# A long convolution with a gated block, forward and backward: transforms moved from dense products on TensorE to a radix-8 transform shared with VectorE, and one row order for all stages

## The chip, the cores and the metric

The kernel runs on one core of a Trainium2 chip. The metric is the device time of one execution in microseconds, taken as the median of several runs. When two kernels are compared, the ratio is the mean time of one kernel's fast runs over that of the other's fast runs of the same rounds on the same chip. It is therefore not quite the ratio of the medians quoted beside it.

## The reference, cut to what matters

Ten outputs: the result and nine gradients. The gradients come from automatic differentiation, so the kernel has to write out the backward pass by hand.

```python
# S = 2048 rows, D = 1024 channels, F = 3584; all bf16
def _A_ref(q, k, v, shift_k, ssm_k, ssm_D):
    k_pad = jnp.pad(k, ((0, 0), (ks - 1, 0), (0, 0)))               # ks = 4
    for t in range(ks):
        k_shift = k_shift + k_pad[:, t:t + S, :] * shift_k[:, ks - 1 - t]
    kv = k_shift * v
    y = irfft(rfft(pad(kv, 2 * S)) * rfft(pad(ssm_k, 2 * S)))[:S]     # long convolution, each channel
    return q * (y + kv * ssm_D)

def _B_ref(x, w_gate, w_up, w_down):
    h = (x @ w_gate) * (x @ w_up)
    return h @ w_down

xn = layernorm(x); s = _A_ref(xn, ...); g = silu(_B_ref(xn, ...))
out = x + s * g                                                       # and all gradients of it
```

Row t of the shifted k needs rows t-3 to t of k, and the gradient needs rows t to t+3.

## The kernel before

The transforms of the long convolution are dense products with tables of sines and cosines. They go through DRAM between forward, product and inverse. This is the inverse:

```python
for dh in range(DH):
    YSh = ys_pool.tile([P, NB2, 2, 2, 512], BF16, name="YSh")
    for gb in range(NB2):
        dma(YSh[:, gb, :, :, :], Psrc_v[gb, :, :, :, sl])
    for ub in range(NB2):
        for par in range(2):
            ps = pspool.tile([P, 512], F32, name="psI")
            for gb in range(NB2):
                for c in range(2):
                    nc.tensor.matmul(ps[:], tws2[c][:, gb * P:(gb + 1) * P], YSh[:, gb, par, c, :], ...)
```

Transposes go to one bank eight at a time, but each 128-column block is copied out by itself:

```python
for i in range(nt):
    nc.tensor.transpose(pst[:, i * P:(i + 1) * P], srcs[g0 + i], ident[:])
for i in range(nt):
    nc.any.tensor_copy(dst_fn(g0 + i), pst[:, i * P:(i + 1) * P])
```

For the shift, k is first copied to a padded array in DRAM. Each of the four taps is then its own load, shifted by a row, and each covers 128 partitions:

```python
nc.sync.dma_start(out=KPAD[0:4, :], in_=zero_bf[0:4, :])
for sb in range(NB):
    dma(KPAD[4 + sb * P:4 + (sb + 1) * P, :], kin[sb * P:(sb + 1) * P, :])
# ... later, for each block of 128 rows and each tap j:
    kt = dkp.tile([P, D], BF16, name=f"kt2_{j}")
    base_row = 4 + sb * P - j
    dma(kt[:], KPAD[base_row:base_row + P, :])
```

## Time and profile before

| | before |
|---|---|
| time | 3117 us median (3114 to 3120, 4 runs) |
| span of the profiled run | 3117.5 us |
| TensorE busy | 88% |
| VectorE / ScalarE / GpSimd busy | 52% / 34% / 20% |
| bytes moved by DMA | 627 MB in 393,008 packets |

The groups table of the page puts the costliest kinds of instruction first. The columns are line, engine, operation, output and inputs, shapes and count, then busy time and mean ns of one, then the idle time before them and what ended it:

```profile
L429 PE MATMUL psI<-YSh,TWR 128*128 128x512 bf16 x1536 | 355.9, 391 | 69.5 <-DVE TWR L217 19.1
L443 ACT COPY HH<-pst_hh 128x128 bf16<-128x128 bf16 x441 | 117.2, 266 | 50.0 <-PE pst_hh L441 38.0
```

The first line is the inverse transform shown above. It is the largest single group on TensorE, and 69.5 us of waiting come on top. The second is one of the single-block copies, 441 times 0.27 us.

### The profile page before, as it was taken

How to read it: one execution, taken by the hardware profiler on the slowest of the kernel's cores; microseconds unless marked ns; L12 is line 12 of the kernel's file. 1: busy time of each engine (PE TensorE's matmuls, PEld its weight loads, DVE VectorE, ACT ScalarE, POOL GpSimd, SP SyncE). 2: the span in 40 equal slices, each digit the busy share in tenths (PEclk: the TensorE clock that was granted, in tenths of full speed). 3: DMA queues.
4: the chain of work that ended last, by engine and by line, in shares of the span. 5: the costliest groups of instructions: out<-in, count | busy, mean ns of one | idle time of the engine just before them, and what ended most of it. 6: DMA issues, size and time to landing. Idle time of an engine off the chain costs nothing. (4 is left out here: it accounts for less than half of the span.)

```text
span 3117.5 us, 39882 instructions
## 1 busy us (share of the span) xinstructions
PE 2728.1 (88%) x13818; PEld 1281.9 (41%) x13818; DVE 1626.6 (52%) x3829; ACT 1060.1 (34%) x2938; POOL 626.8 (20%) x1049
## 2 busy tenths in 40 slices
PE   4949899999799979799899999878899599889888
PEld 2413344444344434444444444433444344444333
DVE  7977778111255751299953331184997460034461
ACT  6512433333101113545535543300555530242222
POOL 2221132222334320112110110133221111112200
PEclk8978999999899989899999999998999689889988
DMA  7795595343748882588644432266875685558602
GB/s 250 286 334 193 193 322 216 145 167 117 280 156 288 284 295 102 185 299 280 214 168 140 141 127 92 94 224 208 296 264 178 213 250 158 161 162 244 210 25 84
DMA packets 393008, 626.92 MB, mean 201 GB/s; under 512 B 147795, under 2 KB 260435, under 8 KB 388964
## 3 DMA queue, kind: packets, MB, share of 16 engines
q1 hardware_dynamic: 304406, 312.36, 30.9%
q0 software_dynamic: 88400, 312.02, 27.9%
q8 instruction: 108, 1.77, 0.2%
q14 instruction: 94, 0.77, 0.1%
HBM read 406.89 MB, written 221.55 MB: 202 GB/s over the span
## 5 line engine op out<-in xcount | busy, mean ns | idle before, releaser
L429 PE MATMUL psI<-YSh,TWR 128*128 128x512 bf16 x1536 | 355.9, 391 | 69.5 <-DVE TWR L217 19.1
L688 PE MATMUL psG<-XNT,wg_s 128*128 128x512 bf16 x896 | 342.7, 383 | 11.3 <-ACT g_b L691 6.8
L689 PE MATMUL psU<-XNT,wu_s 128*128 128x512 bf16 x896 | 342.6, 382 | 3.2 <-DMA wu_s<-in_B_w_up_dram 3.0
L1105 PE MATMUL ps_dxn<-WGT,dgt_l 128*128 128x512 bf16 x896 | 341.6, 382 | 0.0
L1105 PE MATMUL ps_dxn<-WUT,dut_l 128*128 128x512 bf16 x896 | 340.9, 381 | 0.2 <-DMA dut_l<-DUTd 0.2
L936 PEld LDWEIGHTS <-XNR 128*128 128x128 bf16 x1792 | 174.9, 98 | 212.7 <-issue 9.1
L429 PEld LDWEIGHTS <-TWR 128*128 128x128 bf16 x1536 | 152.2, 100 | 262.0 <-issue 64.5
L920 PE MATMUL ps_dh<-DBMT,WDT 128*128 128x512 bf16 x896 | 221.3, 390 | 9.8 <-ACT WDT L443 8.7
L1058 PE MATMUL ps_dwd<-DBM,HH 128*128 128x512 bf16 x896 | 206.2, 382 | 12.1 <-ACT HH L443 7.4
L936 PE MATMUL ps_dw<-DG,XNR 128*128 128x512 bf16 x896 | 199.9, 381 | 3.9 <-ACT w_b L939 3.0
L756 PE MATMUL ps_bm<-WD,ht_t 128*128 128x512 bf16 x896 | 195.7, 381 | 3.7 <-DMA ht_t<-HTd 3.7
L936 PE MATMUL ps_dw<-DU,XNR 128*128 128x512 bf16 x896 | 194.9, 379 | 1.6 <-ACT w_b L939 1.5
L695 DVE TENSOR_TENSOR h_b<-g_b,u_b 128x512 bf16<-128x512 bf16 x112 | 47.4, 423 | 225.6 <-ACT u_b L693 225.6
L939 ACT CAST w_b<-ps_dw 128x512 bf16<-128x512 f32 x112 | 65.3, 584 | 267.3 <-PE ps_dw L936 257.7
L691 ACT CAST g_b<-psG 128x512 bf16<-128x512 f32 x112 | 65.5, 585 | 256.4 <-PE psG L688 239.7
L689 PEld LDWEIGHTS <-wu_s 128*128 128x128 bf16 x896 | 88.3, 99 | 117.7 <-issue 10.8
L688 PEld LDWEIGHTS <-wg_s 128*128 128x128 bf16 x896 | 88.2, 98 | 112.3 <-issue 8.7
L443 ACT COPY HH<-pst_hh 128x128 bf16<-128x128 bf16 x441 | 117.2, 266 | 50.0 <-PE pst_hh L441 38.0
L756 PEld LDWEIGHTS <-ht_t 128*128 128x128 bf16 x896 | 87.7, 98 | 111.7 <-issue 4.6
L1105 PEld LDWEIGHTS <-dut_l 128*128 128x128 bf16 x896 | 88.0, 98 | 106.6 <-issue 1.6
L1105 PEld LDWEIGHTS <-dgt_l 128*128 128x128 bf16 x896 | 88.1, 98 | 105.2 <-issue 1.1
L1058 PEld LDWEIGHTS <-HH 128*128 128x128 bf16 x896 | 84.7, 98 | 110.8 <-ACT HH L443 15.2
(341 smaller groups left out, 4574.9 us busy)
## 6 DMA issues: line engine op xcount, KB each, us to landing
kt<-KPAD SPq DMA_DIRECT2D x64, 256.0 KB, 5.2
kt<-KPAD POOLq DMA_DIRECT2D x64, 256.0 KB, 5.0
dgt_l<-DGTd SPq DMA_DIRECT2D x16, 896.0 KB, 11.5
dut_l<-DUTd POOLq DMA_DIRECT2D x16, 896.0 KB, 8.8
dgt_l<-DGTd POOLq DMA_DIRECT2D x16, 896.0 KB, 8.4
dut_l<-DUTd SPq DMA_DIRECT2D x16, 896.0 KB, 8.1
KVFd<-kvf_t POOLq DMA_DIRECT2D x6, 1536.0 KB, 6.0
pp_kvf<-KVFd SPq DMA_DIRECT2D x12, 768.0 KB, 9.7
```

The source lines that it names most:

```text
L429: nc.tensor.matmul(ps[:], tws2[c][:, gb * P:(gb + 1) * P], YSh[:, gb, par, c, :], start=(i_mm == 0), stop=(i_mm == nmm - 1))
L443: nc.any.tensor_copy(dst_fn(g0 + i), pst[:, i * P:(i + 1) * P])
L688: nc.tensor.matmul(psG[:], wg_s[:, dc, fi * P:(fi + 1) * P], rhs, start=(dc == 0), stop=(dc == DC - 1))
L689: nc.tensor.matmul(psU[:], wu_s[:, dc, fi * P:(fi + 1) * P], rhs, start=(dc == 0), stop=(dc == DC - 1))
L691: nc.scalar.copy(out=g_b[:], in_=psG[:])
L695: nc.vector.tensor_tensor(h_b[:], g_b[:], u_b[:], ALU.mult)
L756: nc.tensor.matmul(ps[:, dh * 512:(dh + 1) * 512], lhsT, WD[:, fc, dh * 512:(dh + 1) * 512], start=(fc == 0), stop=(fc == FC - 1))
L920: nc.tensor.matmul(ps[:], WDT[:, ddc, fi * P:(fi + 1) * P], DBMT[:, ddc, cs], start=(ddc == 0), stop=(ddc == DC - 1))
L936: nc.tensor.matmul(ps[:], XNR[:, sb, dc * P:(dc + 1) * P], src[:, sb, :], start=(sb == 0), stop=(sb == NB - 1))
L939: nc.scalar.copy(out=w_b[:], in_=ps[:])
L1058: nc.tensor.matmul(pss[k][:, dh * 512:(dh + 1) * 512], HH[:, sb, fi * P:(fi + 1) * P], DBM[:, sb, dh * 512:(dh + 1) * 512], start=(sb == 0 ...
L1105: nc.tensor.matmul(ps[:], lt[:, fc, :], wt[:, fc, :], start=(i_acc == 0), stop=(i_acc == n_acc - 1))
```

## The change

The intent: take TensorE's largest non-essential work away. Rows are ordered as (half c, partition u, r of 8), so that a transform of length 4096 splits into a dense product over u (128x128 matmuls, on TensorE) and a radix-8 butterfly over r (on VectorE). All stages use that order, so nothing is reordered between them. Eight transposes fill a bank and leave it in one copy. Transforms are interleaved with dense products by a pump that hands out work in proportion. The diff has some 2,000 lines. Its core:

```diff
-    def fwd_transform2(Zs, tw_source, pspool, on_acc, on_nyq):
-        ...  nc.tensor.matmul(psA[:], twc_t[:, ub * P:(ub + 1) * P], rhs, ...)     # 512 columns
+    def fwd_unit(x, X, wp, psp, nr=2):                    # 128 channels, all 2048 rows
+        W = wp.tile([P, 20, 256], F32, name="W")
+        for h in range(4 // nr):
+            ...  nc.tensor.matmul(ps[:, 2 * i + k, g * P:(g + 1) * P], TF[:, r0 + i, c, k, ...],
+                                  x[:, 8 * c + r0 + i, :], ...)                     # 128 columns
+            nc.scalar.copy(out=s, in_=psS[:])
+            tt(W[:, n * h:n * h + n, :], s, psP[:], ADD)
+            tt(W[:, 8 + n * h:8 + n * h + n, :], s, psP[:], SUB)
+        dft_even(W, 0, W[:, 16:20, :], X, False)          # VectorE
+        dft_odd(W, 8, W[:, 16:18, :], X, False)           # VectorE
...
-            for i in range(nt):
-                nc.any.tensor_copy(dst_fn(g0 + i), pst[:, i * P:(i + 1) * P])
+            for dc in range(DC):
+                nc.tensor.transpose(ps[:, dc, :], x4[:, i, dc * P:(dc + 1) * P], ident[:])
+            nc.any.tensor_copy(XNT[q][:, :, i * P:(i + 1) * P], ps[:])
...
-        for sb in range(NB):
-            dma(KPAD[4 + sb * P:4 + (sb + 1) * P, :], kin[sb * P:(sb + 1) * P, :])
+                k = kst.tile([P, 11, 256], BF16, name="k")     # 8 rows and a halo of 3
+                if c == 0:
+                    V.memset(k[0:1, 0:3, :], 0.0)
+                    ld(k[0:1, 3:11, :], kin[0:8, d0:d0 + 256].rearrange("(o r) d -> o r d", o=1))
+                    ld(k[1:P, :, :], bass.AP(kin.tensor, kin.offset + 5 * D + d0,
+                                             [[8 * D, P - 1], [D, 11], [1, 256]]))
+                else:
+                    ld(k[:], bass.AP(kin.tensor, kin.offset + 1021 * D + d0, [[8 * D, P], [D, 11], [1, 256]]))
...
+    def dk_unit(ds, ew, psy):                              # in the w_down gradient, eight times
+        ld(kh[1:P, 0, :, :], bass.AP(kin.tensor, kin.offset + 5 * D + d0, [[8 * D, P - 1], [D, 11], [1, P]]))
+        ld(dk[0:P - 1, :, 8:11, :], src[1:P, :, 0:3, :])
...
+            nc.scalar.activation(hv[:, 2 * rp:2 * rp + 2, :], ps[:], ACT.Copy, scale=WSC)   # step of 16 bytes
```

## The prediction

> **What bounds the kernel now.** I read the page first (engine shares, the forty slices), then the table of busy time by stage with stage borders taken from the first and last start of each matmul line, then the timeline of TensorE and of VectorE for the price of one instruction. The page says:
>
> ```profile
> PE 2728.1 (88%) x13818; PEld 1281.9 (41%) x13818; DVE 1626.6 (52%) x3829; ACT 1060.1 (34%) x2938; POOL 626.8 (20%) x1049
> PE 24%; issue 8%; ACT 4%; DMA 4%; DVE 3%; POOL 1%; SPq 0%; POOLq 0%; ACTq 0%; DVEq 0%
> ```
>
> TensorE is the bound, but busy time counts overlapping pipeline ends, so I price it from the timeline instead:
>
> ```profile
> 1607.53 27.79 PE L936 MATMUL ps_dw<-DU,XNR 128*128 128x512 bf16 x128
> 1635.15 1.06 PE L441 MATMUL pst_fg<-ident,wrow 128*128 128x128 bf16 x16
> ```
>
> One 512-column matmul lasts 0.379 us alone, so 128 of them start every (27.79-0.38)/127 = 0.2158 us. A 128-column one lasts 0.219, so sixteen start every (1.06-0.22)/15 = 0.056 us. By the kernel's own order it issues about 11,270 of the first (3,168 of them in the transforms) and 2,528 of the second: 2,432+142 = 2,574 us of pure streaming in a span of 3,118. The other 544 us are waits and a slow clock, and the stage table shows where (columns: stretch, its length, busy time of PE, PEld, DVE, ACT, POOL, then granted clock, DMA share, GB/s):
>
> ```profile
> 188.00:245.00 57.00, 9.00 (x20) 2.13 (x21) 32.82 (x55) 1.15 (x2) 15.13 (x29) 0.52 0.97 358
> 390.00:800.00 410.00, 395.14 (x1824) 178.45 (x1823) 158.52 (x386) 128.54 (x248) 110.56 (x191) 0.98 0.53 189
> 940.00:1137.00 197.00, 195.57 (x896) 87.67 (x896) 136.86 (x195) 32.31 (x31) 70.75 (x132) 0.99 0.81 283
> 1297.00:2018.00 721.00, 678.05 (x3867) 331.08 (x3865) 381.94 (x1233) 334.46 (x1096) 99.00 (x166) 0.98 0.52 175
> 2437.00:2480.00 43.00, 17.89 (x117) 11.81 (x116) 22.56 (x69) 22.54 (x80) 8.65 (x10) 0.61 0.93 313
> ```
>
> The second, third and fourth rows are dense stages: 1,792 matmuls (387 us) in 410, 896 (193 us) in 197, and 643 us of work in 721. The first and last are seams, where TensorE starves while a DRAM round trip or weight transposes catch up. Six such seams sum to about 190 us. The first also shows DMA saturating at 358 GB/s, a number needed below.
>
> **What the Trainium skill says.** "TensorE: Matmul & The Clock Gate", section "Back-to-back issue gap", gives N/2.4 + 2.5 ns for a warm stream: 216 and 56 ns for 512 and 128 columns, and it adds that real load-and-multiply pairs of 128 columns take about 81 ns. The trace agrees with the first (215.8, 56) and not with the 81. For 256 columns, which the trace lacks, the formula gives an estimate of 109 ns. "VectorE: DVE Perf Modes", section "The perf-mode tier table (the rule you actually need)", lets a two-tensor operation on bf16 run at 2x and on f32 at 1x. The trace agrees (start to start 0.60 and 1.14 us for 1,024 elements):
>
> ```profile
> 2200.54 0.69 DVE L996 TENSOR_TENSOR dkprod<-dksh,Wbc 128x1024 bf16<-128x1024 bf16 x1
> 2201.14 1.22 DVE L1008 TENSOR_TENSOR acc<-acc,prodf 128x1024 f32<-128x1024 f32 x1
> 2202.28 0.69 DVE L997 TENSOR_TENSOR dkacc<-dkacc,dkprod 128x1024 bf16<-128x1024 bf16 x1
> ...
> 23.03 1.28 DVE L217 SCALAR_TENSOR_TENSOR twc_g<-S0n,SPHp,tw_tmp 128x1024 bf16<-128x1024 f32 x1
> 24.23 1.28 DVE L220 SCALAR_TENSOR_TENSOR tws_g<-C,SPHn,tw_tmp 128x1024 bf16<-128x1024 f32 x1
> ```
>
> "DMA: Bandwidth & Descriptors", section "Where 436 GB/s comes from", puts the HBM limit of one core near 358 GB/s; the saturated stretch above shows the same figure.
>
> **The change, TensorE.** The transforms go from 3,168 matmuls of 512 columns (684 us) to 1,536 forward and 1,024 inverse ones of 128 columns and 256 of 256 columns: 143+28 = 171 us. Added are 128 small matmuls for the gradient of D (7) and 128 full ones for that of the shift kernel (28). The transposes of the saved h disappear (448), but h is now transposed when it is made (448), so their number hardly moves. The dense products stay at 8,064 matmul equivalents. New total: 7,296x0.2158 + 2,048x0.109 + 5,152x0.056 = 1,575+224+288 = 2,087 us. So 487 us of streaming leave, and the seams of DRAM round trips between transforms go with them. Single-block evictions of transposes (0.27 us each on ScalarE, some 1,700) become evictions of eight (about 1.06 us per eight), so ScalarE stays under TensorE everywhere.
>
> **VectorE.** It inherits the transform. With the spacings above (0.60 us for 512 f32, 1.14 for 1,024, 2.2 for 2,048; estimates scaled: 0.40 for 256-element scalar-tensor-tensor, 1.13 for 2,048 bf16), a forward unit costs 4x1.14 + 2x1.14 + 4x0.60 + 6x0.60 + 8x0.40 + 0.3 for direct dependences = 16.3 us. An inverse costs 16.2 and a product 6.9 to 7.5.
>
> **Stages, as the build's own order shows them.** (The order is interleaved by a scheduler, so I count per stage.)
>
> First stage: layer norm, gate and up products, both forward transforms and the first inverse. TensorE: 387 + 86 (conv) + 43 (transposes) = 516 us. VectorE: eight slices of 2x16.3+6.9+16.2+2.3 = 58 us, 464 in all; shift products 64x1.13 = 73; 56 h products 34; layer norm 36; tables 18; rest 6: 631. So this stage turns from TensorE-bound to VectorE-bound. The waits: 12 us until the first operands are there; per forward unit about 2.5 us, as its work tile and its two PSUM banks are single and ScalarE's 1.0 us copy stands between matmul and add, 16 times = 40; ScalarE's queue in front of it, some 17. Sum 700 us. In the order, the last h product stands before more than a whole slice of conv work, so about 80 us at the end are VectorE alone. TensorE can put only one block of the next stage there.
>
> Middle stage: w_down product, gates, elementwise, half of the dy transforms. TensorE 193+7+14 = 215 less 16 done before; VectorE 16x6.9 + 4x16.5 = 176; but the bytes are 29.4 (h) + 7.3 (w_down) + 16.8 + 4.2 + 16.8 + 6 = 81 MB, at 358 GB/s 226 us. I take 235.
>
> Gradient stage: dh 196, dw 387, transposes 70, conv 55 = 708 us of TensorE; VectorE has 628 us over this and the next part, so it is beside. The dense stage before ran 12% over its content, mostly transposes in single blocks. I allow 9%, for the single A and B buffers whose loads come late in each of the 14 slabs: 770, plus 15 for the seam in front. Then dw_down: 193+14+28 = 235, I take 240.
>
> Last stage: 387+25, 20 for the first 7.5 MB of loads (5.5 MB of transposed gradients are queued before the first weights; at 358 GB/s 21 us), 13 for the tail of the last block: 445.
>
> Sum 700+235+785+240+445 = 2,405. For clock ramps and unplaced waits (seams cost 190 us before, I have named 35 here) I add 35: **2,440 us**, 22% less.
>
> **Rivals.** (1) The first stage locks step: VectorE waits for TensorE in queue order and TensorE for VectorE, and starved TensorE drops to half clock, as at 188 to 245 us (0.52). For it: single-buffered PSUM and work tiles. Against: the order has already moved other work into many of the gaps. It would cost 16x6 = about 100 us more: 2,540. (2) The scheduler's order hides all waits: first stage 660, gradient stage 735: 2,340 or a little below. (3) The middle stage and gradient stage are DMA-bound by small pieces: 256- and 512-byte runs in the new layouts. For it: 81 MB in 230 us is already the ceiling, and the kernel before moved its 627 MB with a third of its packets under 512 B. Against: the new h blocks are 14 KB per partition. 10% less rate costs 25 us there: 2,465. (4) VectorE's transform costs more than it saves, and nothing is gained: this would need VectorE's instructions to be twice as long as measured. I give this almost nothing.
>
> **Range and chances.** Rivals 1 and 2 span 2,340 to 2,540; waits I have not thought of make the upper side longer: 2,330 to 2,590. Faster by over 2% 0.98, within 2% 0.01, slower 0.01.
>
> **What would show it.** Right: total DVE near 1,480 us (631+176+628+50), VectorE 85 to 95% busy in the first 700 us with TensorE near 75% and a granted clock under 0.9 there; a stretch of 60 to 90 us before the first w_down products with TensorE nearly idle; 512-column matmuls still 0.379 us; TensorE over 90% from then on. Wrong: VectorE under 80% busy in the first stage (rival 1), DMA share at 0.95 in the middle stage with TensorE waiting for the h blocks (rival 3), or TensorE waits on the gate product in each gradient slab over 8 us.

## More of the kernel before

One more view, which the prediction did not read: the load queue at the start (start, duration, queue, line, operation, output and input, count). It shows how the kernel before gets at the shifted k.

```profile
2.07 5.84 SPq L68 DMA_DIRECT2D KPAD<-in_A_k_dram  x8
10.14 1.93 SPq L68 DMA_DIRECT2D kt<-KPAD  x2
```

These entries are the time for which the queue is taken up by issuing. Eight copies of k occupy it for 5.84 us, two shifted loads for 1.93 us. Nothing is held up for long.

## The result, and the profile after

The changed kernel takes 2807.65 us median (2797.88 to 2811.73, 4 runs), with 3117.07 us for the kernel before in the same rounds. The ratio of the fast runs is 0.9001, 95% interval 0.8979 to 0.9023. It is faster, but by 10% and not by 22%: 367.65 us above the 2,440 that I had predicted, and outside the range.

The page says:

```profile
PE 2217.0 (79%) x14506; PEld 1222.7 (44%) x14506; DVE 1545.0 (55%) x2273; ACT 870.6 (31%) x1141; POOL 587.7 (21%) x972
issue 29%; POOL 2%; PE 2%; DVE 0%; DMA 0%; ACT 0%; POOLq 0%; ACTq 0%
```

TensorE has lost 511 us of busy time and the span only 315. So TensorE, 88% busy before, is 79% busy now: it waits more. The chain of the second line covers about a third of the span, and most of that is unexplained issue, so this time it doesn't help. The stages do. The view below has the columns of the one in the prediction; its last row lies inside the first.

```profile
0.00:866.00 866.00, 591.07 (x4208) 328.75 (x4209) 635.79 (x892) 310.54 (x450) 153.49 (x281) 0.88 0.47 162
866.00:1075.00 209.00, 197.70 (x1171) 98.01 (x1169) 157.09 (x244) 54.78 (x67) 71.00 (x101) 1.00 0.88 315
1075.00:1109.00 34.00, 6.34 (x54) 5.49 (x55) 10.59 (x23) 3.25 (x4) 6.40 (x9) 0.50 1.02 237
1109.00:1934.00 825.00, 743.12 (x5686) 472.13 (x5685) 480.51 (x727) 344.39 (x439) 300.06 (x486) 0.99 0.55 177
1934.00:2299.00 365.00, 249.74 (x1121) 112.34 (x1119) 137.35 (x230) 70.61 (x71) 42.73 (x72) 0.88 0.39 111
2299.00:2370.00 71.00, 14.15 (x57) 6.66 (x58) 21.44 (x36) 3.10 (x4) 5.39 (x7) 0.61 0.52 163
2370.00:2802.00 432.00, 414.84 (x2216) 199.29 (x2214) 102.25 (x123) 83.97 (x107) 8.67 (x16) 0.99 0.36 124
5.00:43.00 38.00, 5.10 (x9) 0.69 (x7) 0.38 (x1) 5.26 (x9) 0.00 (x0) 1.00 0.22 55
```

The rows in order: first stage (866 us, I had said 700), middle stage (209, I had said 235), its seam and the gradient stage (34+825, I had said 785), the w_down gradient and the gap after it (365+71, I had said 240), last stage (432, I had said 445). So the first stage and the w_down gradient are where the time is. In both, TensorE's clock falls to 0.88 and no engine is full. In the w_down gradient, TensorE is busy for 250 us of 365, VectorE for 137, and the DMA share is 0.39. That is the picture of a wait, not of a bound. The last row shows the first wait: for 38 us VectorE does 0.38 us of work and the DMA engines are 22% busy.

Most of the prices in the prediction held (TensorE's and then VectorE's timeline: start, duration, engine, line, operation, shapes, count):

```profile
1559.77 13.33 PE L630 MATMUL psdw<-dgu,XN 128*128 128x512 bf16 x61
1584.93 7.04 PE L609 MATMUL psdh<-wdt,DBMT 128*128 128x256 bf16 x63
1594.40 0.59 PE L630 MATMUL psdw<-dgu,XN 128*128 128x512 bf16 x2
1595.01 0.61 PE L620 MATMUL tr<-ident,dgu 128*128 128x128 bf16 x8
```

```profile
406.12 2.13 DVE L161 TENSOR_TENSOR W<-W 128x512 f32<-128x512 f32 x3
408.17 2.77 DVE L164 SCALAR_TENSOR_TENSOR HX<-W 128x256 bf16<-128x256 f32 x8
```

Sixty-one 512-column matmuls in 13.33 us are (13.33-0.38)/60 = 0.216 us apart, and 63 of 256 columns are 0.109 apart, taking 0.27 for one alone: (7.04-0.27)/62. The eight scalar-tensor-tensor steps of 256 elements take 2.77 us, about 0.34 apart, where I had estimated 0.40. The three additions of 512 f32 elements take 2.13 us, about 0.7 apart, where I had priced 0.60.

So the extra time is not in the work, but in what it waits for. Lines picked from the table of waits (engine and what waits <- for what: us in total, times, longest):

```profile
DVE dka L161 <- DMA dkh<-DKSHd: 215.7, 8, 30.4
DVE acc L161 <- DMA k<-in_A_k_dram: 113.3, 3, 43.0
PE psY L718 <- DMA dkh<-DKSHd: 110.4, 7, 33.2
PE psY L681 <- ACT hr L684: 41.2, 24, 1.9
```

The first three are loads, and the loads are those of k and of the gradient of the shifted k, each with its halo. (VectorE and TensorE wait for the same loads in the first and the third line, so these two are not to be added.) What the load queue does with them:

```profile
5.25 2.19 SPq L57 DMA_DIRECT2D k<-in_A_k_dram  x2
7.49 35.51 SPq L57 DMA_DIRECT2D v<-in_A_v_dram  x1
43.04 1.91 SPq L57 DMA_DIRECT2D hrow<-in_A_ssm_k_dram  x1
45.08 0.82 SPq L57 DMA_DIRECT2D x<-in_A_q_dram  x2
...
2093.35 25.00 SPq L57 DMA_DIRECT2D kh<-in_A_k_dram  x3
2118.45 9.48 SPq L57 DMA_DIRECT2D dkh<-DKSHd  x3
```

The load of v right after k sits in the queue for 35.51 us, and the rows of the impulse response and of x stand behind it. In the w_down gradient the shift unit shown occupies the queue for 25.00+9.48 us; the eight take 32 to 36 us each, 270 us in all. And VectorE's first product on k comes late (VectorE's timeline):

```profile
47.57 1.22 DVE L161 TENSOR_TENSOR acc<-k,Wbc 128x2048 bf16<-128x2048 bf16 x1 [42.19 <-DMA k<-in_A_k_dram]
```

### The profile page after: what moved, and what is told of

Same layout as the page of the kernel before. It is cut to its first block, busy times and chain, and to the rows that moved or that the text cites. A ratio compares the mean times of both kernels' runs of the same rounds, so it can differ in the third digit from the quotient of the medians.

```text
span 2802.4 us, 36132 instructions
## 1 busy us (share of the span) xinstructions
PE 2217.0 (79%) x14506; PEld 1222.7 (44%) x14506; DVE 1545.0 (55%) x2273; ACT 870.6 (31%) x1141; POOL 587.7 (21%) x972
## 5 line engine op out<-in xcount | busy, mean ns | idle before, releaser
L369 PE MATMUL psg<-wslab,XNT 128*128 128x512 bf16 x1792 | 421.3, 385 | 3.2 <-ACT gu L371 3.2
L630 PE MATMUL psdw<-dgu,XN 128*128 128x512 bf16 x1792 | 405.0, 380 | 9.4 <-DVE dgu L161 8.2
L161 DVE TENSOR_TENSOR W<-W 128x512 f32<-128x512 f32 (+1 forms) x384 | 315.5, 822 | 7.3
L845 PEld LDWEIGHTS <-dgut 128*128 128x128 bf16 x1792 | 174.5, 98 | 207.0 <-DMA dgut<-DGUTd 0.8
L630 PEld LDWEIGHTS <-XN 128*128 128x128 bf16 x1792 | 172.1, 98 | 198.5 <-issue 11.4
L369 PEld LDWEIGHTS <-XNT 128*128 128x128 bf16 x1792 | 172.1, 99 | 186.1 <-issue 13.6
L793 PE MATMUL psdw<-DBMT,dgu 128*128 128x512 bf16 x896 | 204.7, 386 | 22.4 <-ACT wb L796 15.0
L609 PE MATMUL psdh<-wdt,DBMT 128*128 128x256 bf16 x1792 | 217.1, 274 | 1.0 <-ACT DBMT L598 0.9
L509 PE MATMUL psbm<-wd,ht 128*128 128x512 bf16 x896 | 201.4, 383 | 6.9 <-ACT bm L511 2.6
L609 PEld LDWEIGHTS <-DBMT 128*128 128x128 bf16 x1792 | 171.2, 98 | 20.9 <-ACT DBMT L598 2.0
```

The costliest lines, as they stand in the source:

```text
L161: V.tensor_tensor(o, a, b, op)
L369: nc.tensor.matmul(ps[:], XNT[q][:, dc, i * P:(i + 1) * P], w[:, dc].rearrange("p a f -> p (a f)"), start=(dc == 0), stop=(dc == DC - 1))
L509: nc.tensor.matmul(ps[:], ht[:, fc, i * P:(i + 1) * P], wds[fc // 4][:, fc % 4, :], start=(fc == 0), stop=(fc == NF - 1))
L609: nc.tensor.matmul(ps[:, i, :], DBMT[:, dc, b * P:(b + 1) * P], wdt[:, dc, :], start=(dc == 0), stop=(dc == DC - 1))
L630: nc.tensor.matmul(ps[:].rearrange("p a f -> p (a f)"), XN[:, b, dc * P:(dc + 1) * P], dgus[b // 4][:, b % 4].rearrange("p a f -> p (a f)" ...
L793: nc.tensor.matmul(ps[:], hs[b // 4][:, b % 4, fi // 2, (fi % 2) * P:(fi % 2 + 1) * P], DBM[:, b, dh * 512:(dh + 1) * 512], start=(b == 0) ...
```

## The experiments

**Theory A.** The halo of row 0 is zero, so the load of k for the first half leaves out partition 0 and covers 127 partitions. The Trainium skill, "DMA: Bandwidth & Descriptors", section "Why a DMA increments its semaphore by 16 and not by 1", says that a transfer is spread over the largest number of engines up to 16 that divides the size of the slowest dimension of its access patterns, here the partition count, and names 127 partitions as a case of one engine. 127 is a prime. All three loads with `P - 1` or `1:P` are such cases, and the in-order queue waits behind them.

**Rivals.** B: the runs of 256 and 512 bytes make these loads slow, whatever the partition count. C: the load may be long, but only the queue standing behind it costs time. D: the shift units are serial because their tiles are single-buffered.

### e1_split_all, e2_split_first, e3_split_down: cut the loads in 112 and 15 partitions

```diff
-ld(k[1:P, :, :], bass.AP(kin.tensor, kin.offset + 5 * D + d0, [[8 * D, P - 1], [D, 11], [1, 256]]))
+ld(k[16:P, :, :], bass.AP(kin.tensor, kin.offset + 125 * D + d0, [[8 * D, 112], [D, 11], [1, 256]]))
+ld(k[1:16, :, :], bass.AP(kin.tensor, kin.offset + 5 * D + d0, [[8 * D, 15], [D, 11], [1, 256]]))
# e1 and e3: kh[1:P] likewise, and
-ld(dk[0:P - 1, :, 8:11, :], src[1:P, :, 0:3, :])
+ld(dk[0:112, :, 8:11, :], src[1:113, :, 0:3, :])
+ld(dk[112:P - 1, :, 8:11, :], src[113:P, :, 0:3, :])
```

e2 cuts only the first of the three places, e3 only the other two.

> All three loads that cover 127 partitions are cut in two, 112 and 15 partitions; bytes and run lengths stay. Theory A (a load over 127 partitions runs on one DMA engine of sixteen, and the in-order load queue stands behind it): the first load of k lands by about 15 us instead of 47, each shift-kernel unit loses its 24+9 us, the stretch of w_down gradient goes from 365+71 us to about 260+30, the first stage loses 25 to 60 us; total about 2,600 us (2,540 to 2,680). Rival B (the runs of 256 and 512 bytes are slow however many partitions there are): no change, 2,790 to 2,820.

> Only the four loads of k in the first stage are cut in 112 and 15 partitions. Theory A: the first stage gains 25 to 60 us and nothing else moves, total 2,745 to 2,785. Rival B: 2,790 to 2,820. The gains of this run and of e3_split_down should add up to that of e1_split_all.

> Only the loads of the shift-kernel units late in the w_down gradient are cut (k with its halo, and the halo of the gradient). Theory A: first stage unchanged at about 866 us, w_down gradient plus its tail falls by about 150 us, total about 2,650 (2,620 to 2,690). Rival B: 2,790 to 2,820. Rival D (the units are serial because their tiles are single-buffered, not because of the loads): less than 40 us gained, 2,770 or more.

Measured: e1 2535.03 us (ratio to the kernel before 0.812, interval 0.8101 to 0.8139), e2 2676.56 us (0.8581), e3 2657.73 us (0.8521). All are correct. The gains over the changed kernel's 2807.65 are 273, 131 and 150 us, and 131+150 = 281 against 273 for both: they add up. Rivals B and D fall. e3 came out within its range; e1 is 5 us better than the lower end of its range. For e2 I expected 25 to 60 and got 131, because I had counted only the first of the four loads of k in full. The waits table had it: 113 us of waits on k. The first stage of e1 and its last three stretches read:

```profile
0.00:738.00 738.00, 590.38 (x4200) 328.57 (x4201) 634.81 (x892) 310.18 (x450) 152.26 (x280) 0.92 0.56 189
984.00:1812.00 828.00, 746.57 (x5688) 474.87 (x5687) 479.80 (x726) 344.83 (x439) 300.04 (x486) 0.99 0.55 176
1812.00:2068.00 256.00, 229.41 (x1113) 108.09 (x1111) 139.02 (x234) 70.67 (x72) 43.45 (x73) 1.00 0.59 165
2068.00:2101.00 33.00, 12.75 (x60) 6.23 (x59) 18.68 (x33) 2.38 (x3) 4.84 (x6) 0.66 1.00 312
130.00:628.00 498.00, 462.93 (x3406) 257.96 (x3405) 463.60 (x633) 219.03 (x315) 128.66 (x234) 0.97 0.59 202
```

Same work, 128 us less in the first stage and 147 less in the w_down gradient with its gap; the gradient stage in between hasn't moved. The last row is inside the first stage: VectorE is now 463.60 of 498 us busy, 93%. So is TensorE, with 462.93. The shares don't tell which of the two is the bound there.

### e9_cut_126 and e10_cut_122: how much does the partition count do?

A cut in two makes the transfer shorter as well as rounder. So the same loads were cut in 126+1 and in 122+5. By the rule 126 = 14x9 has fourteen engines, 122 = 2x61 has two.

```diff
-ld(k[1:P, :, :], bass.AP(kin.tensor, kin.offset + 5 * D + d0, [[8 * D, P - 1], [D, 11], [1, 256]]))
+ld(k[6:P, :, :], bass.AP(kin.tensor, kin.offset + 45 * D + d0, [[8 * D, 122], [D, 11], [1, 256]]))
+ld(k[1:6, :, :], bass.AP(kin.tensor, kin.offset + 5 * D + d0, [[8 * D, 5], [D, 11], [1, 256]]))
```

> The same three loads are cut in 126 partitions and 1. If the number of engines is the largest divisor up to 16 of the partition count (126 = 14x9, so 14 engines), this is as good as 112 and 15: the first product on k starts near 15 us, total 2,525 to 2,560. If only counts that are multiples of 16 spread out, the load stays on one engine and nothing is gained: 2,780 to 2,820.

> The same three loads are cut in 122 partitions and 5. By the divisor rule 122 = 2x61 gives two engines: the first product on k starts near 30 us (47 with one engine, 15 with sixteen), a shift unit's loads hold the queue some 17 us instead of 33, and the total lies between the two, 2,620 to 2,700. If any cut does, because the queue only dislikes one long transfer: 2,525 to 2,560.

Measured: e9 2532.13 us (0.8127), e10 2640.89 us (0.8474). The first product on k in e1, e9 and e10, in this order (VectorE's timeline):

```profile
14.99 1.23 DVE L161 TENSOR_TENSOR acc<-k,Wbc 128x2048 bf16<-128x2048 bf16 x1 [9.46 <-DMA k<-in_A_k_dram]
```

```profile
14.62 1.23 DVE L161 TENSOR_TENSOR acc<-k,Wbc 128x2048 bf16<-128x2048 bf16 x1 [9.37 <-DMA k<-in_A_k_dram]
```

```profile
29.26 1.23 DVE L161 TENSOR_TENSOR acc<-k,Wbc 128x2048 bf16<-128x2048 bf16 x1 [23.99 <-DMA k<-in_A_k_dram]
```

By the rule, sixteen engines give 14.99, fourteen 14.62, two 29.26, and one, in the changed kernel, 47.57. The load queue goes the same way: with 122 partitions the loads of k hold it for 19.11 us, where in the changed kernel they and the v behind them held it for 2.19+35.51.

```profile
5.35 19.11 SPq L57 DMA_DIRECT2D k<-in_A_k_dram  x3
```

The cut as such doesn't do it: 126+1 and 122+5 are both two transfers. The divisor does: the four partition counts fall in the order of the rule, and 112 and 126 are alike. The share of busy DMA engines shows their number too, in stretches in which hardly anything but this load moves. Here are the changed kernel, e10, and the kernel e4 of the next section, in which the load is whole (columns as in the stage table):

```profile
20.00:40.00 20.00, 0.00 (x0) 0.00 (x0) 0.00 (x0) 0.00 (x0) 0.00 (x0) 1.00 0.07 20
12.00:24.00 12.00, 1.74 (x3) 0.20 (x2) 0.00 (x0) 2.00 (x4) 0.00 (x0) 1.00 0.14 40
20.00:44.00 24.00, 0.00 (x0) 0.00 (x0) 0.00 (x0) 0.00 (x0) 0.00 (x0) 1.00 0.07 20
```

One of sixteen engines would be a share of 0.06, and two 0.13. The readings are 0.07 and 0.14, and the rate doubles with them, from 20 to 40 GB/s.

### e4_act_queue: the loads whole, but in another queue

```diff
-ld(k[1:P, :, :], bass.AP(...))
+nc.scalar.dma_start(out=k[1:P, :, :], in_=bass.AP(...))      # likewise kh[1:P, 0]
```

> The two loads of k over 127 partitions stay whole, but ScalarE's queue issues them, so that the other loads no longer stand behind them; the halo of the gradient stays on the old queue. Rival C (only the queue behind the load matters, the load's own length does not): nearly the gain of e1_split_all, 2,580 to 2,680. Theory A (the load itself is long, its consumer waits 24 to 35 us wherever it is issued): the product that takes k still starts near 45 us and the shift units still take over 25 us each, so about half the gain or less, 2,690 to 2,790.

Measured: 2865.84 us (0.9188), 58 us slower than the changed kernel, outside all the ranges above. The half gain that I had expected from theory A didn't come. The product on k still starts at 46.49 us, although the load was issued at 0.74 us: the load is as long in this queue. But the edit did not free the old queue, so it is no clean test of rival C. The old queue's own waits show that it stood until these very loads had landed (engine and what waits <- for what: us in total, times, longest):

```profile
SPq L57 <- DMA kh<-in_A_k_dram: 139.7, 8, 21.7
SPq L57 <- DMA k<-in_A_k_dram: 99.3, 3, 40.0
```

How much of the cost is the length of the load itself, and how much the queue behind it, stays open. In the w_down gradient it got worse, and the old queue shows how:

```profile
2098.50 20.84 SPq L57 DMA_DIRECT2D dgu<-Hd  x8
...
2184.42 20.66 SPq L57 DMA_DIRECT2D dgu<-Hd  x8
```

These eight plain loads of h take the queue for 20.8 us, and 6.1 to 6.8 us in e1. One of the long loads of kh was in flight meanwhile: it was issued at 2076.47 us, and TensorE got it at 2115.62. It fits that the loads of h need all sixteen engines and one of them is occupied by the long load. That last step is argued, not shown. Either way, issuing from another queue did not get the other loads past the long one.

### e5_hr_flat, e6_hr_dve, e11_hr_pool: the copy with a step of 16 bytes

With the loads mended, 95 us are left over my prediction. The last line of the waits table above is a suspect: TensorE waits 41 us, 24 times, for ScalarE's copy of the impulse-response gradient out of PSUM. That copy writes bf16 elements 16 bytes apart. The Trainium skill, "SBUF — State Buffer", section "Door 1: The DMA port swizzle (why `[64,N]` ≈ `[32,N]`)", says that SBUF has 16-byte lines and that an access which changes the line each time pays a penalty. It gives no figure. All three kernels are e1 plus:

```diff
-nc.scalar.activation(hv[:, 2 * rp:2 * rp + 2, :], ps[:], ACT.Copy, scale=WSC)
# e5: the same 512 elements side by side (that output is wrong, on purpose)
+nc.scalar.activation(hr_flat[:, 512 * rp:512 * rp + 512], ps[:].rearrange("p a b -> p (a b)"), ACT.Copy, scale=WSC)
# e6: VectorE with the step
+V.tensor_scalar(hv[:, 2 * rp:2 * rp + 2, :], ps[:], WSC, None, op0=MUL)
# e11: ScalarE side by side into a new tile, GpSimd reorders it later
+nc.scalar.activation(hb[:, 2 * rp:2 * rp + 2, :], ps[:], ACT.Copy, scale=WSC)
+nc.gpsimd.tensor_copy(hv[:, 2 * rp:2 * rp + 2, :], hb[:, 2 * rp:2 * rp + 2, :])
```

> On top of e1_split_all: ScalarE writes the impulse-response gradient contiguously instead of with a step of 16 bytes (wrong values in that one output, on purpose). Theory: the stepped write is what makes the copy 2.44 us; it falls to about 0.6, TensorE's 42 us of waits on it go, and as TensorE is the bound there the total falls by 30 to 42 us, to 2,490 to 2,505. Rival: the waits lie beside other waits and are given back: 2,525 to 2,540.

> On top of e1_split_all: VectorE instead of ScalarE does that copy with its 16-byte step, values right. If the step is dear only on ScalarE: about 0.65 us each and nearly the gain of e5_hr_flat, 2,490 to 2,515. If VectorE pays for the step as well (2 us or more each): TensorE waits as before, 2,525 to 2,545.

> On top of e1_split_all: ScalarE copies the impulse-response gradient out of its bank contiguously (0.6 us) and GpSimd does the reordering with the 16-byte step from SBUF afterwards, values right. Theory: TensorE is released after 0.6 us as in e5_hr_flat, total 2,490 to 2,505, whatever GpSimd takes as long as it is under some 8 us each (16 us between units). Rival: GpSimd's step is so slow that its stores pile up: 2,530 or more.

Measured: e5 2495.39 us (0.8008), that output wrong and the others right; e6 2534.43 us (0.813), correct; e11 2499.34 us (0.8019), correct. The line of the copy (count, then shortest/median/longest in ns, first and last start) in e1, e5 and e6:

```profile
L685 ACT ACTIVATE hr<-psY x32: 2434/2439/2470, 1623.5 to 1938.6; 128x512 bf16<-128x512 f32 x32
```

```profile
L685 ACT ACTIVATE hr<-psY x32: 597/597/597, 1621.8 to 1901.7; 128x512 bf16<-128x512 f32 x32
```

```profile
L685 DVE TENSOR_SCALAR hr<-psY x32: 2412/2424/2453, 1625.0 to 1941.8; 128x512 bf16<-128x512 f32 x32
```

The step costs a factor of four on ScalarE, and VectorE with the step takes as long. That points to the step of the write and not to ScalarE, but VectorE side by side was not run. TensorE is busy for 90% of this stage, and removing its 42 us of waits was worth 40 us of time by the medians, 35 by the ratios. In e11 GpSimd takes 2.74 us for each reorder; e11's time can't be told from e5's, so the gain stays, and the values are right.

### e7_late_tr: the transposes of the gate gradients one block later

```diff
             dgus.append(dh_quad(sl, q, wdt))
+            if q > 0:
+                dgu_transposes(sl, q - 1, dgus[q - 1])    # was inside dh_quad, right after the product
```

> On top of e1_split_all: the transposes of each block of gate gradients are emitted one block later, so that TensorE has other products between the VectorE product and the transposes that need it. Theory: the gradient stage is over my estimate because TensorE waits for that product (24 us at the transposes, 9 at the weight gradient) and for the copies between (10); most of it goes, 25 to 40 us, total 2,495 to 2,510. Rival: the scheduler had placed them as well as it could, and the waits move elsewhere: 2,520 to 2,545.

Measured: 2518.72 us (0.8084), correct. The gain is 16 us by the medians and 11 by the ratios, between theory and rival. TensorE's 24 us of waits on the product in front of the transposes are gone, but its wait on the copy that frees the single transpose bank went from 10 to 23 us. So the waits were real, and half of them came back as the next one in the row.

### e8_h_pool: the product h on GpSimd

If the first stage is bound by VectorE, work taken from it should shorten the stage.

```diff
-tt(h[:], gu[:, :, 0, :], gu[:, :, 1, :], MUL)
+nc.gpsimd.tensor_tensor(h[:], gu[:, :, 0, :], gu[:, :, 1, :], MUL)
```

> On top of e1_split_all: GpSimd instead of VectorE makes the 56 products h of the first stage (0.69 us each on VectorE, some 34 us in all). If the first stage is bound by VectorE's own work: it gets 20 to 35 us shorter, total 2,500 to 2,515. Rival: GpSimd takes over 2 us each or slows VectorE while it runs, or its stores come later: no gain or a loss, 2,530 to 2,580; VectorE's 1,024-element bf16 product would then be longer than 0.69 us.

Measured: 2651.34 us (0.8496), correct, and 116 us slower than e1. The rival is right in direction, but the loss is far larger than its 2,530 to 2,580. The groups of e8, and then the second of them in e1 (columns as in the table before):

```profile
L374 POOL TENSOR_TENSOR h<-gu 128x1024 bf16<-128x1024 bf16 x56 | 193.3, 3452 | 2.2 <-PE tr L379 1.4
L161 DVE TENSOR_TENSOR W<-HX 128x2048 f32<-128x2048 bf16 x16 | 44.2, 2801 | 0.2
```

```profile
L161 DVE TENSOR_TENSOR W<-HX 128x2048 f32<-128x2048 bf16 x16 | 36.0, 2295 | 0.1
```

GpSimd takes 3.45 us where VectorE took 0.69, and VectorE's own operations get longer while it runs: 2.80 instead of 2.30 us here. VectorE lost 38.6 us of products, and its busy time still rose from 1543.4 to 1588.7 us. The Trainium skill, "SBUF — State Buffer", section "SBUF: two separate sides", says that VectorE's operations with two SBUF inputs and GpSimd's exclude each other at a shared port. The trace agrees in direction: GpSimd's work made VectorE's instructions longer. It also shows which ones. Additions of 1,024 f32 elements with both inputs in SBUF went from 1.22 us to 1.33 on average, and those with one input in PSUM stayed at 1.22. A full exclusion of one by the other is not shown. The experiment doesn't tell what the first stage would gain if VectorE really had less to do.

### e13_pace, e12_combo, e14_combo_pace

e13 is e1 with the transform work of the first stage handed out 15% faster, e12 is e1 with e7 and e11 together, e14 is both.

```diff
-            pump((4 * sl + q + 1) / (4.0 * NSL))
+            pump(1.15 * (4 * sl + q + 1) / (4.0 * NSL))
```

> On top of e1_split_all: the transform work of the first stage is handed out 15% faster than the gate and up products, so that it ends nearer to them. If the 107 us at the end of the stage, in which VectorE runs nearly alone, are lost time: up to 25 us shorter, 2,505 to 2,520. If the whole stage is bound by VectorE's 635 us of work, the tail only moves forward: 2,525 to 2,545, with the tail shorter and the part before it longer.

> e7_late_tr and e11_hr_pool together on top of e1_split_all. If their waits are different ones they add up (15 and 36 us): total 2,475 to 2,490. If both only move the same wait: 2,495 or more. It should also be the fastest right kernel so far.

> e12_combo and e13_pace together. Different stages, so the sum of the two changes within 8 us: 2,465 to 2,490.

Measured: e13 2538.93 us (0.814, interval 0.8126 to 0.8154), e12 2477.09 us (0.7946, interval 0.7933 to 0.7959), e14 2482.06 us (0.796). All are correct. e13 is no faster than e1. The edit didn't even do what it was meant to: the scheduler put the last gate products 12 us earlier instead of later, and the stretch behind them grew from 110 to 120 us with the stage's end where it had been, at 736 us. So the expected shape was wrong. The constant end speaks for VectorE's work as the bound, but it is weak evidence, because the tail was not made shorter. e12's gains add up (e7's 16 and e11's 36 us alone, 58 together), and it is the fastest correct kernel: 20.5% less than the kernel before, and 0.7946/0.9001 = 0.883 of the changed one. Its gradient stage and its w_down gradient:

```profile
984.00:1774.00 790.00, 741.91 (x5626) 479.60 (x5682) 489.90 (x726) 312.40 (x439) 338.84 (x502) 0.98 0.58 184
1774.00:2012.00 238.00, 228.89 (x1096) 109.49 (x1117) 139.04 (x235) 42.06 (x72) 81.34 (x89) 0.99 0.64 178
```

## Why the prediction was right or wrong

The stages side by side, in us. Seams are counted with the stage that follows, except the gap after the w_down gradient, which is counted with it:

| stage | predicted | changed kernel | e1 (loads cut) | e12 |
|---|---|---|---|---|
| first | 700 | 866 | 738 | 737 |
| middle | 235 | 209 | 209 | 210 |
| seam and gradient | 785 | 859 | 865 | 827 |
| w_down gradient and gap | 240 | 436 | 289 | 269 |
| last | 445 | 432 | 432 | 432 |
| unplaced | 35 | | | |
| sum | 2,440 | 2,802 | 2,533 | 2,475 |

**TensorE's content: right.** The prices of 512 and 256 columns held, and the middle and the last stage were 26 and 13 us better than predicted. I counted 81 MB in the middle stage, but 315 GB/s times 209 us are 66: the rest moved outside the stage.

**VectorE's work: right in the sum.** The first stage has 635.79 us of it, and I had 631. In total it is 1,545 against 1,480, 4% more. Most of that is in the last stage, 102 us where I had 50; the middle stage has 157 where I had 176.

**The step that failed: "The waits: 12 us until the first operands are there", and with it the first stage's waits of 69 us and "Then dw_down: 193+14+28 = 235, I take 240".** Both treat loads as free unless bytes are short. The first operands came after 42 us of waiting, and three more loads of k were as slow. In the w_down gradient eight shift units held the queue for 32 to 36 us each, 270 us in all, more than the stage's own 235. Cutting the loads so that the partition count has a large divisor gave back 273 of the 367 us and put the kernel at 2,535. That is inside the range that I had given, but only because its upper side was wide: it is 95 us above the point. I had opened the page that states the rule, and read only its bandwidth. The `P - 1` stood in the diff.

**The sign for rival 1 appeared, and its cause did not.** I had written that VectorE under 80% busy in the first stage would mean that TensorE and VectorE lock step over single buffers. It was 635.79 of 866, 73%, with a clock of 0.88. But e1 keeps all the single buffers, takes 128 us less for the stage, and has VectorE at 93% in the middle of it. A low busy share shows that something is waited for, not what.

**Rival 3 fell.** The DMA share of 0.88 in the middle stage cost nothing against my sum. Rival 4 fell as well, and rival 2's 2,340 was not reached by any run.

**The gradient stage: content right, reason for the allowance wrong.** I allowed 9% over a content of 708 us for "the single A and B buffers", and it took 825 us plus a seam of 34 where I had 15. The A and B loads made VectorE wait (85 us for B in e1), but VectorE has room there. The terms that were missing are TensorE's waits on the 16-byte-step copy, which e5 shows to be worth about 40 us over this stage and the next, and on the gate product with its transpose bank, of which e7 got 16 at most. With both mended the stage is 790. The sign that I had named, over 8 us of waits on the gate product in each slab, did not appear: they are 32 us over 14 slabs.

**What stays open.** The first stage is 38 us over its 700 in e1. VectorE's 635 us of work hardly leave a shorter way, but TensorE is as busy in the middle of the stage, and neither e8 nor e13 removed work from VectorE cleanly. That the stage is bound by VectorE is likely and not shown. About 20 us of transpose-bank waits remain in e12. So does the seam of 37 us.

## What to carry to other kernels

Look at the partition count of every load before the byte count: leaving out a single partition for a border turned three kinds of small loads into the costliest waits of the kernel, and cutting them in two gave back more than any other edit here. When no engine is full and the DMA share is low, read the load queue, and look at what stands in it just in front of the entry that takes long. And check the step of what is written to SBUF: an output order that scatters neighbouring elements by 16 bytes made the copy four times as long on ScalarE and no shorter on VectorE, and cost nothing measurable when GpSimd, which had time, did the reordering later.

## What the Trainium skill lacked or had wrong

- "DMA: Bandwidth & Descriptors" has the rule of the partition count, and this agrees: the first product on k came at 47.57 us with 127 partitions, 29.26 with 122, 14.62 with 126, 14.99 with 112. What it lacks is a measured case: one such load of 0.7 MB went at 20 GB/s with a DMA share of 0.07, and the entry behind it stood in the queue for 35.5 us.
- "SBUF — State Buffer" has the 16-byte line without a figure for the writes of ScalarE or VectorE. Here 512 bf16 elements written 16 bytes apart from PSUM took 2.44 us on ScalarE and 2.42 on VectorE, against 0.60 side by side on ScalarE.
- "SBUF — State Buffer" has the shared port of VectorE and GpSimd. The size: 56 products on GpSimd took 3.45 us each instead of 0.69, a VectorE operation beside them 2.80 instead of 2.30, and the kernel was 116 us slower.
- "TensorE: Matmul & The Clock Gate" gives about 81 ns for real pairs of loading and multiplying 128 columns. In a run of sixteen they started 56 ns apart here (1.06 us), in the kernel before. The same passage gives about 131 ns for 512 columns; here 128 of them in 27.79 us started 216 ns apart.
